# Loads of k and q ahead of the centroids, a cleared tile for the first idle products, and a shorter norm

## The chip, the cores and the metric

The kernel runs on one core of a Trainium2 chip. TensorE (PE), VectorE (DVE), ScalarE (ACT), GpSimd (POOL) and SyncE (SP) each take their own list of instructions in order and wait for each other through semaphores. The metric is the device time of one execution in microseconds, as a median over runs; less is better.

## What is computed

Clustered attention, followed by two dense blocks. Each query and key is assigned to the centroid whose direction is nearest; a query attends only to keys of its own cluster.

```python
B, H, S, D = 2, 8, 768, 64          # 16 clusters per head
c_n = centroids / (norm(centroids) + 1e-06)
q_assign = argmax(einsum('bhsd,hcd->bhsc', q_n, c_n))    # k_assign the same way
mask = q_assign[:, :, :, None] == k_assign[:, :, None, :]
scores = where(mask, q @ k.T / sqrt(D), -1e9)
x = softmax(scores) @ v             # then heads side by side: 1536 x 512
x = leaky(x @ moe_w_in) @ moe_w_out         # max(0.01 h, h)
x = relu(x @ moe2_w_in)**2 @ moe2_w_out
```

## The kernel before

Inputs come two heads at a time: a pair p holds q and k as tiles `rqk` (128 partitions: two heads of 64 dimensions; 768 columns) and v as `rv`. There are 8 pairs. Matrix products run in fp32 split into a rounded part and the rest, so that three products make one. Attention runs in units of 256 queries; the order of all engines in the attention is written out by hand in strings such as `RAMP` (the start) and `PLAN` (the steady part). The dense blocks follow, where TensorE has work all the time.

The change lies in the first microseconds, before `RAMP` begins. In the order of the program:

- GpSimd makes the identity `ident`, small constants (`eps`, `msc`, `mbi`, written at lines 156 to 166), a bf16 copy `identb` (L168), the cleared block tile `cbd` (L170), the ranks `desc` and padding.
- SyncE loads the centroids `ct` (L326), then k, q of pair 0 and q, k of pair 1 (`loads_qk`, L323, four transfers of 384 KB), then v (L318) and five copies between on-chip tiles (L694).
- `warm_up(9)` puts nine idle 128x128 products of `ident` on TensorE (L331); their result is not used. An fp32 product is two passes on TensorE, so nine of them show as 18.
- `prep_centroids` norms the centroids: squares and sums on VectorE (L335, L337), the square root on ScalarE (L339, behind a load of its function table), a load of the table for exp with a dummy step (L340), then on VectorE a floor of 1e-30 (L341), a reciprocal, one refining step and the scaling of `ct` (L343 to L351). TensorE transposes `ct` (L353), and ScalarE copies the two halves into `cbd` (L355, L356).
- `warm_up(3)` puts three more idle products behind the transpose.
- `head_0` makes the split operands of head 0 from k and q on VectorE and ScalarE (L712 to L729; `hb`). Then `RAMP` begins: `dK` and `dQ` multiply k and q with `cbd` (`dots`, L391, six products each), `fill` adds idle products (L774), `choose` finds each row's best cluster on VectorE (L782, L785, tile `pads`), `mask_mm` transposes that (L799, `ohT`), and the scores S (L521) follow.

All engines' order in this part is that of the code.

Of the kernel before, what the change touches and what calls it, by code (L numbers as in the profile page):

```python
# [8 lines left out]
F32 = mybir.dt.float32  # L9
# [5 lines left out]
AF = mybir.ActivationFunctionType  # L15
ALU = mybir.AluOpType
# [87 lines left out]
def attention_moe_moe_kernel(  # L104
# [9 lines left out]
    nc = tc.nc  # L114
# [35 lines left out]
    const = ast.enter_context(tc.tile_pool(name="const", bufs=1))  # L150
    const.tile([128, 120], F32, name="cpad")

    ident = const.tile([128, 128], F32, name="ident")
    make_identity(nc, ident)
    eps = const.tile([128, 1], F32, name="eps")
    nc.gpsimd.memset(eps, 1e-9)
    msc = const.tile([128, 1], F32, name="msc")
    mbi = const.tile([128, 1], F32, name="mbi")
    nc.gpsimd.memset(msc[0:32], BIG)
# [7 lines left out]
    identb = const.tile([128, 128], BF16, name="identb")  # L167
    nc.gpsimd.tensor_copy(out=identb, in_=ident)  # L168
    cbd = const.tile([128, HP, 2 * C], F32, name="cbd")
    nc.gpsimd.memset(cbd, 0.0)  # L170
    desc = const.tile([128, 24, C], F32, name="desc")
    for c in range(C):
        nc.gpsimd.memset(desc[:, :, c], float(2 ** (C + 8 - c)))
# [149 lines left out]
            nc.sync.dma_start(out=rqks[p][:, j], in_=qk[p, j])  # L323

    ct = const.tile([128, D], F32, name="ct")
    nc.sync.dma_start(out=ct, in_=cen)  # L326

    def warm_up(n):
        w = ps_t.tile([128, 512], F32, tag="T", name="warm")
        for i in range(n):  # L330
            nc.tensor.matmul(out=w[:, 0:128], lhsT=ident, rhs=ident, start=True, stop=True)  # L331

    def prep_centroids():
        sq = const.tile([128, D], F32, name="sq")
        nc.vector.tensor_tensor(out=sq, in0=ct, in1=ct, op=ALU.mult)  # L335
        ss = const.tile([128, 1], F32, name="ss")
        nc.vector.tensor_reduce(out=ss, in_=sq, axis=AX.X, op=ALU.add)  # L337
        n0 = const.tile([128, 1], F32, name="n0")
        nc.scalar.activation(out=n0, in_=ss, func=AF.Sqrt)  # L339
        nc.scalar.activation(out=const.tile([128, 1], F32, name="tab"), in_=eps, func=AF.Exp)  # L340
        nc.vector.tensor_scalar(out=n0, in0=n0, scalar1=1e-30, scalar2=None, op0=ALU.max)  # L341
        rn = const.tile([128, 1], F32, name="rn")
        nc.vector.reciprocal(out=rn, in_=n0)  # L343
        nc.vector.scalar_tensor_tensor(
            out=n0, in0=ss, scalar=rn, in1=n0, op0=ALU.mult, op1=ALU.add
        )
        nc.vector.tensor_scalar(
            out=n0, in0=n0, scalar1=0.5, scalar2=1e-6, op0=ALU.mult, op1=ALU.add
        )
        nc.vector.reciprocal(out=rn, in_=n0)  # L350
        nc.vector.tensor_scalar(out=ct, in0=ct, scalar1=rn, scalar2=None, op0=ALU.mult)  # L351
        ctp = ps_t.tile([128, 512], F32, tag="T", name="ctp")
        nc.tensor.transpose(ctp[0:64, 0:128], ct, ident)  # L353
        cview = ctp[0:64, 0:128].rearrange("p (a h c) -> p a h c", h=2, c=C)
        nc.scalar.copy(out=cbd[0:64, :, 0:C], in_=cview[:, :, 0])  # L355
        nc.scalar.copy(out=cbd[64:128, :, C : 2 * C], in_=cview[:, :, 1])  # L356
# [336 lines left out]
    for h, j in ((2, 3), (0, 2), (0, 3), (1, 2), (1, 3)):  # L693
        nc.sync.dma_start(  # L694
            out=heads[h][80:128, j].bitcast(F32), in_=heads[2][80:128, 2].bitcast(F32)
        )
    warm_up(9)
    prep_centroids()
    eighth = const.tile([128, 1], F32, name="eighth")
    warm_up(3)  # L700

    for h in range(2):
        hbs[h] = heads[h]
# [206 lines left out]
    for op in RAMP.split():  # L910
        if ":" in op:
            name, i = op.split(":")
            step(name, int(i), unit_ops[name])
        elif "@" in op:
            name, i = op.split("@")
# [6 lines left out]
    for u in range(-1, NU + 5):  # L922
# [9 lines left out]
        for op in PLAN[u % UPP].split():  # L932
            if ":" in op:
                name, lag = op.split(":")
                i = u - int(lag)
                if 0 <= i < NU:
                    step(name, i, unit_ops[name])
            else:
                name, ahead = op.split("@")
# [6 lines left out]
        w = u - (NU - UPP)  # L946
# [610 lines left out]
```

## Time and profile before

| what | value |
|---|---|
| median of 3 runs | 733.88 us (733.5 to 734.03) |
| profiled execution | 734.87 us, its span 733.1 us |
| TensorE busy | 725.6 us, 99% of the span |
| chain that ended last | TensorE 91%, VectorE 4%, ScalarE 2%, GpSimd 1% |

The span is the time from the first to the last instruction of the profiled execution. The chain is followed back from the last instruction: at each step to what released it, or to the instruction ahead on its engine. A start time in the rows counts from the span's start.

### The profile page before, as it was taken

The numbers are of one execution on the slowest core, as the hardware profiler recorded it, in microseconds if no ns is written. First come the engines' busy times: TensorE is split into PE (matmuls) and PEld (weight loads), VectorE is DVE, ScalarE is ACT, GpSimd is POOL, SyncE is SP. The second block draws the span as 40 slices with busy tenths as digits, with TensorE's granted clock in tenths as the row PEclk, the third lists the DMA queues.
The fourth block names the chain that finished last, engine by engine and source line by source line (L and its number), as shares of the span: only waits on it lengthen the run. The fifth ranks groups of instructions, "written<-read, shape, count | busy, mean of one in ns | idle before, by whom it ended". The sixth has DMA issues, their size and how long they took to land.

```text
span 733.1 us, 11920 instructions
## 1 busy us (share of the span) xinstructions
PE 725.6 (99%) x4246; PEld 644.4 (88%) x4246; DVE 562.3 (77%) x893; ACT 500.0 (68%) x923; POOL 596.5 (81%) x562
## 2 busy tenths in 40 slices
PE   9999999999999999999999999999999999999997
PEld 8999999999998888888888888888888898888986
DVE  7989999999998737686776866887677595775946
ACT  7978988988998777447365464658847558375561
POOL 6999999999959977987787877899798786787840
PEclk9999999999999999999999999999999999999999
DMA  5693573662611312212121131111113112121004
GB/s 150 161 219 104 128 172 104 136 167 66 146 54 59 115 58 79 94 58 97 56 79 57 58 115 58 59 58 58 58 59 114 59 58 79 64 89 57 1 1 173
DMA packets 17756, 65.58 MB, mean 89 GB/s; under 512 B 3120, under 2 KB 6320, under 8 KB 12704
## 3 DMA queue, kind: packets, MB, share of 16 engines
q1 hardware_dynamic: 17696, 64.81, 30.0%
q8 instruction: 34, 0.56, 0.3%
q14 instruction: 26, 0.21, 0.1%
HBM read 43.02 MB, written 3.15 MB: 63 GB/s over the span
## 4 chain that ended last, share of the span: by engine, by line
PE 91%; DVE 4%; ACT 2%; POOL 1%; issue 1%; DMA 1%; ACTq 0%; DVEq 0%; POOLq 0%
PE h L1043 33%; PE o L1274 18%; PE h L1274 10%; PE A L618 8%; PE S L521 7%; PE T L583 7%; PE o L1121 4%; PE S L391 2%; DVE nm L543 1%; ACT e L553 1%; DVE el L600 1%; PE warm L331 1%; DMA out<-q 1%; POOL e L570 0%; PE dots L391 0%
## 5 line engine op out<-in xcount | busy, mean ns | idle before, releaser
L1043 PE MATMUL h<-xh,wh 128*128 128x512 f32 x272 | 106.7, 392 | 0.0
L1043 PE MATMUL h<-xh,wl 128*128 128x512 f32 x272 | 106.1, 390 | 0.0
L1043 PE MATMUL h<-xl,wh 128*128 128x512 f32 x272 | 106.1, 390 | 0.0
L1228 POOL TENSOR_TENSOR gl<-t,gh 128x512 fp32r<-128x512 f32 x56 | 79.9, 1444 | 31.9 <-ACT gh L1225 21.9
L197 POOL TENSOR_TENSOR wl<-ws,wh 128x1024 fp32r<-128x1024 f32 x28 | 67.8, 2420 | 41.8 <-ACT wh L194 41.8
L570 POOL TENSOR_SCALAR e<-e,r 128x768 f32<-128x768 f32 x96 | 87.4, 919 | 12.5 <-PE T L583 6.8
L600 DVE TENSOR_TENSOR el<-T,eh 128x512 fp32r<-128x512 f32 x144 | 94.6, 683 | 3.0 <-ACT eh L594 1.9
L543 DVE TENSOR_REDUCE nm<-S 128x1 f32<-128x768 f32 x96 | 90.9, 949 | 3.9 <-PE S L391 2.5
L553 ACT ACTIVATE e<-S,nm 128x768 f32<-128x768 f32 x96 | 87.3, 910 | 9.6 <-DVE nm L543 5.8
L521 PE MATMUL S<-hb 128*128 128x384 f32 (+1 forms) x384 | 89.6, 347 | 1.6 <-ACT eh L594 0.4
L594 ACT CAST eh<-T 128x512 fp32r<-128x512 f32 x144 | 79.7, 590 | 9.6 <-PE T L583 9.4
L1173 DVE TENSOR_TENSOR h<-h,q 128x512 f32<-128x512 f32 x42 | 29.4, 699 | 70.6 <-PE h L1043 45.3
L197 POOL TENSOR_TENSOR wl<-wt,wh 128x1024 fp32r<-128x1024 f32 x31 | 75.5, 2434 | 9.6 <-ACT wh L194 8.7
L618 PE MATMUL A<-eh,vv 128*128 128x256 f32 x288 | 80.2, 307 | 0.0
L583 PE MATMUL T<-ident,e 128*128 128x128 f32 x576 | 79.5, 273 | 0.0
L618 PE MATMUL A<-el,vv 128*128 128x256 f32 x288 | 73.0, 283 | 0.0
L583 PEld LDWEIGHTS T<-ident,e 128*128 128x128 f32 x576 | 68.9, 143 | 3.0
L224 ACT ACTIVATE wt<-wraw 128x1024 f32<-128x1024 f32 (+1 forms) x33 | 36.8, 1115 | 47.5 <-POOL ws L286 47.3
L521 PEld LDWEIGHTS S<-hb 128*128 128x128 f32 (+1 forms) x384 | 62.2, 189 | 3.7 <-ACT e L553 1.9
L1228 DVE TENSOR_TENSOR gl<-h,gh 128x512 fp32r<-128x512 f32 x70 | 48.0, 688 | 18.3 <-ACT h L1210 7.9
L1043 PEld LDWEIGHTS h<-xh,wh 128*128 128x128 f32 x272 | 51.1, 188 | 11.6 <-DVE gl L1228 1.1
L1043 PEld LDWEIGHTS h<-xh,wl 128*128 128x128 f32 x272 | 51.0, 188 | 10.6
(202 smaller groups left out, 2088.3 us busy)
## 6 DMA issues: line engine op xcount, KB each, us to landing
wraw<-w SPq DMA_DIRECT2D x32, 1024.0 KB, 4.7
hb<-spl SPq DMA_DIRECT2D x14, 576.0 KB, 4.7
hb<-spl SPq DMA_DIRECT2D x42, 192.0 KB, 5.1
rqk<-qk SPq DMA_DIRECT2D x16, 384.0 KB, 3.7
rv<-v SPq DMA_DIRECT2D x8, 384.0 KB, 3.4
out<-q SPq DMA_DIRECT2D x11, 256.0 KB, 2.2
hb<-st SPq DMA_DIRECT2D x56, 24.0 KB, 2.1
hb<-hb SPq DMA_DIRECT2D x5, 144.0 KB, 7.0
```

The lines of the kernel that those rows point to most:

```text
L197: last_of["wl"] = eng.tensor_tensor(out=wl, in0=t, in1=wh.bitcast(F32), op=ALU.subtract).ins
L521: nc.tensor.matmul(out=s[:, c, 0:HALF], lhsT=hb[0:k, a, i * 128 : (i + 1) * 128], rhs=hb[0:k, b, c * HALF : (c + 1) * HALF], start=(a == 0 ...
L543: last_of["nm", t] = nc.vector.tensor_reduce(out=n, in_=s_t[t][:, :, 0:HALF], axis=AX.XY, op=ALU.max, negate=True).ins
L553: nc.scalar.activation(out=e.rearrange("p (a b) -> p a b", a=2), in_=s_t.pop(t)[:, :, 0:HALF], func=AF.Exp, bias=n_t.pop(t), scale=1.0, ac ...
L570: last_of["norm"] = nc.gpsimd.tensor_scalar(out=e_t[t], in0=e_t[t], scalar1=r_t[t // 2][:, t % 2 : t % 2 + 1], scalar2=1.0, op0=ALU.mult, ...
L583: nc.tensor.transpose(T[:, o : o + 128], e_t[2 * u + b][:, kc * 128 : (kc + 1) * 128], ident)
L594: last_of["eh", u, g] = nc.scalar.copy(out=eh[:, 2 * g : 2 * g + 2, :].rearrange("p a b -> p (a b)"), in_=T_t[u, g]).ins
L600: last_of["el"] = last_of["el", u, g] = nc.vector.tensor_tensor(out=el[:, 2 * g : 2 * g + 2, :].rearrange("p a b -> p (a b)"), in0=T_t.pop ...
L618: nc.tensor.matmul(out=A, lhsT=w, rhs=m[:, kc, :], start=(kc == 0 and i == 0), stop=(kc == KC - 1 and i == 1),)
L1043: nc.tensor.matmul(out=out, lhsT=l, rhs=r, start=(first and i == 0), stop=(i == n - 1), skip_group_check=not first,)
L1228: eng.tensor_tensor(out=lo[n], in0=full[n], in1=hi[n].bitcast(F32), op=ALU.subtract)
L1274: nc.tensor.matmul(out=out, lhsT=l, rhs=r, start=(fresh and i == 0), stop=(stop and i == 2), skip_group_check=True,)
```

## The change

The centroids' load is issued by ScalarE, not SyncE, so k and q stand first on SyncE's queue. `cbd` is cleared by VectorE, not GpSimd, and the first two idle products multiply this cleared tile with itself; five with `ident` and three with `identb` (bf16) follow, in place of nine with `ident`. Behind the transpose six bf16 idle products stand in place of three fp32 ones. The floor of 1e-30 under the norm becomes a bias of 1e-30 under the square root, from a new tile `tiny` that GpSimd writes.

```diff
+    tiny = const.tile([128, 1], F32, name="tiny")
+    nc.gpsimd.memset(tiny, 1e-30)
...
-    nc.gpsimd.memset(cbd, 0.0)
+    nc.vector.memset(cbd, 0.0)
+    flat_cbd = cbd.rearrange("p h c -> p (h c)")
...
-    nc.sync.dma_start(out=ct, in_=cen)
-
-    def warm_up(n):
+    nc.scalar.dma_start(out=ct, in_=cen)
+
+    def warm_up(*todo):
         w = ps_t.tile([128, 512], F32, tag="T", name="warm")
-        for i in range(n):
-            nc.tensor.matmul(out=w[:, 0:128], lhsT=ident, rhs=ident, start=True, stop=True)
+        for x, n in todo:
+            for i in range(n):
+                nc.tensor.matmul(out=w[:, 0:128], lhsT=x, rhs=x, start=True, stop=True)
...
-        nc.scalar.activation(out=n0, in_=ss, func=AF.Sqrt)
+        nc.scalar.activation(out=n0, in_=ss, func=AF.Sqrt, bias=tiny)
         nc.scalar.activation(out=const.tile([128, 1], F32, name="tab"), in_=eps, func=AF.Exp)
-        nc.vector.tensor_scalar(out=n0, in0=n0, scalar1=1e-30, scalar2=None, op0=ALU.max)
...
-    warm_up(9)
+    warm_up((flat_cbd, 2), (ident, 5), (identb, 3))
     prep_centroids()
     eighth = const.tile([128, 1], F32, name="eighth")
-    warm_up(3)
+    warm_up((identb, 6))
```

ScalarE at the program's start, before; in brackets the semaphores that a row waits for, by the engine or DMA that raises them:

```order
L339 ACT_TABLE_LOAD
L339 ACTIVATE n_193<-ss 128x1 [waits DVE_49]
L340 ACT_TABLE_LOAD
L340 ACTIVATE tab<-eps 128x1 [waits Pool_49]
L355 COPY cbd<-ctp 64x4x16 [waits PE_49,Pool_49]
```

ScalarE at the same place, now (the lines of the changed kernel stand three or four further down):

```order
L329 DMA ct<-cen 128x64
L343 ACT_TABLE_LOAD [waits DVE_49]
L343 ACTIVATE n_196<-ss,tiny 128x1 [waits Pool_49]
L344 ACT_TABLE_LOAD
L344 ACTIVATE tab<-eps 128x1
L358 COPY cbd<-ctp 64x4x16 [waits PE_49]
```

The centroids' DMA is ScalarE's first instruction, and the wait for VectorE's sum, which stood at the square root, now stands ahead of the table load.

TensorE from its first product to the first dots, before:

```order
L331 MATMUL warm<-ident 128x128 [waits Pool_49]
L331 MATMUL warm<-ident 128x128 x8
L353 MATMUL ctp<-ident,ct 64x128 [waits DVE_49]
L331 MATMUL warm<-ident 128x128 x3
L391 MATMUL dots<-cbd,rqk 128x32 [waits PE_49,DMAHW1_49,Activation_49,Pool_49]
```

TensorE at the same place, now; the two rows on `identb` come three times ahead of the transpose `ctp`, and six times behind it:

```order
L335 MATMUL warm<-cbd 128x128 [waits DVE_49]
L335 MATMUL warm<-cbd 128x128
L335 MATMUL warm<-ident 128x128 [waits Pool_49]
L335 MATMUL warm<-ident 128x128 x4
L335 LDWEIGHTS identb [waits Pool_49]
L335 MATMUL warm<-identb 128x128
...
L356 MATMUL ctp<-ident,ct 64x128 [waits DVE_49]
...
L394 MATMUL dots<-cbd,rqk 128x32 [waits DMAHW1_49,PE_49,Activation_49]
```

The first products wait for VectorE's cleared tile and no longer for GpSimd's identity; in fp32 passes there are 14 ahead of the transpose where there were 18, and three short products.

## Rows read from the trace of the kernel before

**Rows 1.** The page's first and fourth part: busy time, and the chain.

```profile
PE 725.6 (99%) x4246; PEld 644.4 (88%) x4246; DVE 562.3 (77%) x893; ACT 500.0 (68%) x923; POOL 596.5 (81%) x562
PE 91%; DVE 4%; ACT 2%; POOL 1%; issue 1%; DMA 1%; ACTq 0%; DVEq 0%; POOLq 0%
```

**Rows 2.** The chain in order of time, start: start us, us, what.

```profile
1.41 4.21 PE warm L331 x18
5.62 0.21 PE ctp L353
5.84 1.04 PE warm L331 x6
6.88 1.26 PE dots L391 x12
```

**Rows 3.** Timeline of SyncE: start us, us, instruction.

```profile
0.74 0.38 SPq L326 DMA_DIRECT2D ct<-cen  x1
1.17 1.84 SPq L323 DMA_DIRECT2D rqk<-qk  x4
```

**Rows 4.** Timeline of VectorE; in brackets its idle time, and what ended it.

```profile
2.42 0.23 DVE L335 TENSOR_TENSOR sq<-ct 128x64 f32<-128x64 f32 x1 [2.42 <-DMA ct<-cen]
2.68 0.22 DVE L337 TENSOR_REDUCE ss<-sq 128x1 f32<-128x64 f32 x1
3.17 0.15 DVE L341 TENSOR_SCALAR n<-n 128x1 f32<-128x1 f32 x1 [0.27 <-ACT n L339]
3.36 0.16 DVE L343 RECIPROCAL rn<-n 128x1 f32<-128x1 f32 x1
...
4.20 0.26 DVE L351 TENSOR_SCALAR ct<-ct,rn 128x64 f32<-128x64 f32 x1
5.18 0.55 DVE L714 TENSOR_SCALAR hb<-rqk 64x768 fp32r<-64x768 f32 x1 [0.73 <-DMA rqk<-qk]
...
7.23 0.95 DVE L725 SCALAR_TENSOR_TENSOR hb<-rqk,hb 64x768 fp32r<-64x768 f32 x1
8.21 0.36 DVE L782 TENSOR_REDUCE m<-dots 128x12 f32<-128x192 f32 x1
...
9.48 0.84 DVE L782 TENSOR_REDUCE m<-dots 128x12 f32<-128x192 f32 x2
```

**Rows 5.** Timeline of ScalarE.

```profile
0.73 1.28 ACT L339 ACT_TABLE_LOAD   x1 [0.73 <-PEq L1547]
2.94 0.20 ACT L339 ACTIVATE n<-ss 128x1 f32<-128x1 f32 x1 [0.92 <-DVE ss L337]
3.16 1.28 ACT L340 ACT_TABLE_LOAD   x1
4.45 0.20 ACT L340 ACTIVATE tab<-eps 128x1 f32<-128x1 f32 x1
5.93 0.21 ACT L355 COPY cbd<-ctp 64x64 f32<-64x64 f32 x1 [1.28 <-PE ctp L353]
```

**Rows 6.** Timeline of TensorE: weight loads, and the first dots.

```profile
5.21 0.18 PEld L353 LDWEIGHTS ctp<-ident,ct 128*64 128x64 f32 x1
6.72 1.42 PE L391 MATMUL dots<-cbd,rqk 128*128 128x32 f32 x12
```

**Rows 7.** Groups of ScalarE's steps to 18 us: shapes, count | busy us, mean ns.

```profile
L339 ACT ACTIVATE n<-ss 128x1 f32<-128x1 f32 x1 | 0.2, 204 | 0.9 <-DVE ss L337 0.9
L564 ACT ACTIVATE r<-r,eps 128x2 f32<-128x2 f32 x1 | 0.3, 298 | 0.0
```

**Rows 8.** Stretches: busy time by engine, granted clock, DMA engines' busy share, GB/s.

```profile
1.75:2.00 0.25, 0.25 (x2) 0.25 (x2) 0.00 (x0) 0.25 (x1) 0.19 (x3) 1.00 0.51 116
2.00:2.25 0.25, 0.25 (x3) 0.25 (x3) 0.00 (x0) 0.01 (x1) 0.25 (x2) 1.00 0.88 59
...
3.00:3.50 0.50, 0.50 (x5) 0.50 (x3) 0.29 (x2) 0.48 (x2) 0.44 (x8) 1.00 0.74 98
```

**Rows 9.** Timeline of GpSimd: the clearing of the block tile.

```profile
2.17 0.21 POOL L170 MEMSET cbd<- 128x128 f32 x1
```

**Rows 10.** Timeline of TensorE later: three bf16 products.

```profile
27.65 0.33 PE L473 MATMUL ohT<-identb,oh 128*128 128x128 bf16 x3
```

**Rows 11.** Products of one line (ns min/median/max); weight loads 5.6:6.4, 6.6:8.

```profile
L331 PE MATMUL warm<-ident x24: 275/421/582, 1.4 to 6.6; 128*128 128x128 f32 x24
...
L331 PEld LDWEIGHTS warm<-ident 128*128 128x128 f32 x5 | 1.2, 327 | 0.0
...
L391 PEld LDWEIGHTS dots<-cbd,rqk 128*128 128x128 f32 x12 | 1.4, 192 | 0.0
```

**Rows 12.** Waits up to 12.6 us: who for whom, us, times, longest.

```profile
POOL qs L748 <- ACT eighth L729: 4.0, 1, 4.0
```

## The prediction

> **What bounds the kernel now.** I read the page first. TensorE is busy for 99% of the span and carries 91% of the chain of work that ended last [rows 1], so once the pipeline is full nothing outside TensorE can be made late or early by much without the end moving with it. The change touches the first 10 us alone, so the question is what sets the start. The chain in order of time [rows 2] says: idle products from 1.41 to 5.62 us, the centroid transpose, idle products again to 6.88, then the dot products of head pair 0 and the masks. A chain through TensorE's queue names the instruction ahead, even when that one is only padding, so I looked at who was ready when.
>
> Four lanes meet there. (a) The centroids: issued at 0.74, landed 1.7 us later, normed on VectorE from 2.42 to 4.46 with one step on ScalarE between [rows 3 to 5]. (b) TensorE: nine fp32 idle products stand ahead of the transpose, whose weight load starts only at 5.21 [rows 6], 0.75 us after the centroids were ready. That is the loss which the change goes for. (c) k: VectorE's first use of it, L714, starts at 5.18 and waited 0.73 us for its DMA [rows 4]. (d) After that VectorE runs L714, L721, L714, L725 without a gap to 8.18 and reduces the first dots at 8.21 [rows 4]; TensorE's first twelve dot passes end at 6.72 + 1.42 = 8.14 [rows 6]. So VectorE and TensorE arrive together: an edit has to bring both forward to gain, and delays if it pushes back either.
>
> **Part 1, the norm of the centroids.** L341 goes: from its start at 3.17 to the next at 3.36 is **0.19 us saved** [rows 4]. In its place the square root takes its bias from a tile. A ScalarE step on 128x1 without one took 204 ns, L564 with a bias tile took 298 [rows 7]: **+0.09**, bounds 0 and 0.10 since L564 has two elements a row.
>
> The larger cost is in the order of ScalarE's instructions. The square root now waits for two engines (VectorE for the sum, GpSimd for the new tile). Before, the table load L339 stands ahead of any wait, ran from 0.73 to 2.01 and was over 0.92 us before the sum came [rows 5]. In the changed order the wait for VectorE stands ahead of the table load, which can thus start only when the sum is there. The cover of that load was the centroids' transfer; it is gone. Price: **+1.28 us** [rows 5] and about 0.05 for the extra waiting step (this is the idle between neighbours such as 2.90 and 2.94). Part 1 in sum: 1.28 + 0.05 + 0.09 - 0.19 = +1.23. With the centroids landing as before the centroid tile is ready at 4.46 + 1.23 = 5.69 instead of 4.46.
>
> On that load: the row shows 1.28 us, and the step behind the second load starts 0.01 us after it (3.16 + 1.28 = 4.44, then 4.45) [rows 5]. The Trainium skill (ScalarE: Activation LUTs, What ACT_TABLE_LOAD costs) states the same 1283 ns but adds a drain of some 1380 ns for every switch. By that rule the sum would be about 1.4 us longer; no such drain shows here, so I leave it out.
>
> **Part 2, the queues.** SyncE spends 0.43 us between the start of the centroids' DMA and the next one (0.74 to 1.17) [rows 3]. k, q and all behind them go out 0.43 earlier; k lands at about 4.75 instead of 5.18. That is worth 0.43 only while VectorE is free to take it; by part 1 it is not.
>
> The centroids now leave on ScalarE's queue at about 0.73, when its first instruction could start [rows 5], so at the same moment as k, and not ahead of it. No DMA of the trace goes out on ScalarE's queue. Lower bound of the added delay: 0. The centroids' bytes moved before 2.0 us (116 GB/s for a quarter of a microsecond is their 32 KB), and k, issued at 1.17, moved next to nothing until 2.0 [rows 8]; 0.43 earlier it would only begin to. Upper bound: they land with k, 4.75 - 2.4 = 2.3 us late, since the DMA engines are already 74 to 88% busy at 59 to 98 GB/s in several stretches from 2.0 to 3.5 [rows 8], a sign of slow first packets. I take **+0.2**, near the lower end, because the nearest row, the centroids' own transfer, was over before k could have been in its way.
>
> **Part 3, the idle products.** The cleared tile is now written by VectorE as its first work. The trace has no VectorE memset; GpSimd's of the same tile took 0.21 [rows 9], VectorE's step on half as many elements 0.26 [rows 4]. So TensorE begins near 1.0 instead of 1.41. Seven fp32 products are 14 passes; eighteen stood between 1.41 and the transpose's load at 5.21, 0.21 each [rows 6]: until about 4.0. Three bf16 products add 0.3 to 0.65 (later in the kernel three of them span 0.33 [rows 10]; twice that as the other bound, since the fp32 loads are up to 1.7 times slower in this stretch than behind it [rows 11]). TensorE is free for the transpose at 4.3 to 4.6, so this edit does what it says. But the centroid tile is there at 5.7 to 5.9, and TensorE **pauses for over 1 us**.
>
> **The sum.** VectorE: 5.69 + 0.2 = 5.89 plus the usual 0.03 gives L714 at 5.92 against 5.18, +0.74. ScalarE and TensorE: transpose from 5.9; the first product of a row of them takes 0.58 at this clock [rows 11], so the copies into the block tile start at 6.55 instead of 5.93 and the dots at about 7.05 instead of 6.72, +0.3, as six bf16 products (0.3 to 0.65) no longer stand in the way. VectorE is the later of the two. Two reduces at L782 share a row of 0.84 us from 9.48 [rows 4]; the second waits for the second dots, and each lasts 0.36, so some 0.1 to 0.2 us there is waiting that VectorE's delay uses up. That leaves **+0.5 us** at the mask transposes. From there the chain [rows 2] alternates DVE, ACT, POOL and PE with issue gaps of 0.03 to 0.1 and hardly any slack; GpSimd and ScalarE start their own lanes behind the same copies (L748 waits for L729, 4.0 us) [rows 12], so all lanes shift together. I take the whole +0.5 to the end: span 733.6, and against the median, which is 0.99 below the profiled execution's 734.87, 733.88 + 0.5 = **734.4**. Without the 0.2 for the queue 734.2, with 0.6 for it 734.8.
>
> **Rivals.** (1) *The table load is hidden after all*: the chip starts it while the wait is pending. Then the centroid tile is ready at 4.46 - 0.19 + 0.09 + 0.2 = 4.6, the transpose runs at once, dots start at 5.8, and k at 4.75 sets VectorE: -0.43, **733.45**. Against it: the second load, L340, stands behind a step that waited until 2.94 and did not start before 3.16 [rows 5].
> (2) *The centroids queue behind k*: each DMA engine serves both queues in turns, and k's first packets are slow [rows 8]. Taking half to two thirds of the upper bound, they land 1.1 to 1.5 us late in place of 0.2; the sum grows by 0.9 to 1.3, **735.5**. It decides, for a loss over 0.2%, from 1.2 us on. The Trainium skill (DMA: Bandwidth & Descriptors, Queues, rings and completion order) speaks for it: an engine takes packets from its queues by turns. No run so far shows two queues at once.
> (3) *The clock rises later* (slower). The granted-clock column reads 1.00 throughout [rows 8], but the same 128x128 fp32 weight load takes 327 ns in the idle products up to 6.4 us and 192 in the dots behind 6.6 [rows 11]: TensorE ran at the lower level, 1.2 GHz, for some 5 us of work without a pause and then rose to 2.4. With a pause from 4.5 to 5.9 the rise may miss the dots. A pass then takes 0.21 instead of 0.12 (1.42 us for twelve [rows 6]): the first twelve dots cost 1.1 on top of their 0.3, the fills and the second twelve half as much again and more. TensorE then binds instead of VectorE, +1.4 to +2.9 in all: 735.3 to 736.8, **735.7** where the rise falls between the two sets of dots. For it: the pause; against it: TensorE starts 0.4 us sooner and is busy again before 6.6.
> (4) *Absorbed*: some later wait swallows the shift, **733.9**.
>
> **Chances.** Forecast 0.42, (1) 0.10, (2) 0.14, (3) 0.22, (4) 0.12. A measurement can tell about 0.2%, 1.5 us, from no change. Faster by that much needs more than (1) can give: 0.03. Slower by that much is 0.6 of (2), 0.65 of (3) and a tail of the forecast: 0.25. The rest, 0.72, is within. Range 733.2 to 736.0: it holds the forecast, (4), most of (1) and (2) and the cheaper half of (3).
>
> **What would show it.** In the changed profile the first table load should start near 2.95 or later, behind L341's reduce, and not at 0.73; the centroid tile ready at 5.6 to 5.9; TensorE idle for a microsecond or more ahead of the transpose; L717 (now k's first use) waiting for VectorE's own work, not for the DMA; k landed near 4.75. If the table load still stands at 0.73, (1) holds. If the centroids land at 3.4 or later, (2). If the weight loads of the dots take over 300 ns, (3). If L717 is 0.7 late and the exps of the first unit are not, (4).

## The result, and the profile after

The changed kernel takes 740.5 us (median; 739.74 to 741.15) against 733.95 in the same comparison: 1.0085 times as long, 95% interval 1.0074 to 1.0096, or **6.5 us slower**. The forecast was 734.4, +0.5 us, within 733.2 to 736.0, with a chance of 0.72 that the change is too small to be told; the measured time lies far outside. The profiled execution took 739.74 us, with a span of 738.0. It lies only 4.9 us above the profiled one of the kernel before, because that one (734.87) was 0.9 slower than this comparison's median.

The loss is there before the attention has begun. The first row maximum (L543, now L546) starts at 19.88 us instead of 14.00; the first product of the dense blocks is 5.3 us late (234.8 for 229.5 us). These are the two lanes that lead to it, first ScalarE of the changed kernel, from the timeline (start us, us, instruction; idle time and what ended it in brackets), to be held against [rows 5]:

```profile
0.73 0.40 ACTq L329 DMA_DIRECT2D ct<-cen  x1
4.79 1.28 ACT L343 ACT_TABLE_LOAD   x1 [4.79 <-DVE ss L341]
6.09 0.29 ACT L343 ACTIVATE n<-ss,tiny 128x1 f32<-128x1 f32 x1
6.40 1.28 ACT L344 ACT_TABLE_LOAD   x1
...
8.03 0.20 ACT L358 COPY cbd<-ctp 64x64 f32<-64x64 f32 x1
```

The table load waits for VectorE's sum, as its place in the order said, and costs its 1.28 us behind it. But the sum itself is late. VectorE's timeline, against [rows 4]:

```profile
4.23 0.23 DVE L339 TENSOR_TENSOR sq<-ct 128x64 f32<-128x64 f32 x1 [3.23 <-DMA ct<-cen]
4.49 0.22 DVE L341 TENSOR_REDUCE ss<-sq 128x1 f32<-128x64 f32 x1
6.42 0.16 DVE L346 RECIPROCAL rn<-n 128x1 f32<-128x1 f32 x1 [1.71 <-ACT n L343]
...
7.26 0.25 DVE L354 TENSOR_SCALAR ct<-ct,rn 128x64 f32<-128x64 f32 x1
7.43 0.55 DVE L717 TENSOR_SCALAR hb<-rqk 64x768 fp32r<-64x768 f32 x1
...
11.31 0.36 DVE L785 TENSOR_REDUCE m<-dots 128x12 f32<-128x192 f32 x1 [0.90 <-PE dots L394]
```

The centroids land at 4.2 us instead of 2.4. The tile is ready at 7.51 instead of 4.46: 1.81 us for the transfer and 1.25 for the norm. The last row shows a third thing: VectorE, itself over 2 us late, has to wait another 0.9 us for the dots. TensorE's timeline says why, against [rows 6]:

```profile
7.57 0.42 PE L356 MATMUL ctp<-ident,ct 128*64 128x128 f32 x1 [2.84 <-DVE ct L354]
7.78 0.85 PE L335 MATMUL warm<-identb 128*128 128x128 bf16 x6
8.50 2.77 PE L394 MATMUL dots<-cbd,rqk 128*128 128x32 f32 x12
11.08 1.20 PE L777 MATMUL dots<-ident 128*128 128x128 f32 x4
12.08 2.61 PE L394 MATMUL dots<-cbd,rqk 128*128 128x32 f32 x12
...
17.63 0.61 PE L777 MATMUL dots<-ident 128*128 128x128 f32 x4
```

After a stop of 2.84 us the same twelve passes take 2.77 us instead of 1.42, and four fills 1.20; at 17.63 four fills take 0.61 again. The groups of weight loads (count | busy us, mean ns), up to 16.9 us and from 17.6 us on, confirm it with one and the same load:

```profile
L394 PEld LDWEIGHTS dots<-cbd,rqk 128*128 128x128 f32 x24 | 5.3, 332 | 0.1
...
L394 PEld LDWEIGHTS dots<-cbd,rqk 128*128 128x128 f32 x24 | 2.9, 192 | 0.0
```

These 332 ns are the lower level, 1.2 GHz, that [rows 11] show for the idle products (327 ns there), and 192 the upper, 2.4 GHz. The clock rose at about 17.2 us here; in the kernel before it rose at about 6.5. (The granted-clock column reads 1.00 in this whole stretch, although the same load takes 332 ns in one part of it and 192 in the other. So it is the loads that tell the level ahead of the first change that the column shows.)

The chain, in order of time, adds up. Its main pieces, against [rows 2]:

```profile
0.73 3.48 DMA ct<-cen
4.79 1.28 ACT L343
...
8.63 2.64 PE dots L394 x12
11.27 1.01 PE dots L777 x4
12.29 2.40 PE dots L394 x12
14.69 1.01 PE dots L777 x4
15.70 0.64 PE S L524 x2
16.34 1.46 PE ohT L802 x9
...
19.88 0.97 DVE nm L546
```

The last row stood at this place in the chain of the kernel before:

```profile
14.00 0.97 DVE nm L543
```

In the kernel before, the dots were 1.26 each in that chain, so 2.5 us of the 5.9 at the first row maximum lie in the two dozens of dots alone, and the fills, the first scores and the masks lie in the same slow stretch. The transpose starts 2.15 us later (7.57 for 5.42), and its idle products are 0.4 shorter. The rest, 5.9 - 2.15 + 0.4 = 4.1 us, lies in that slow stretch. What remained to be shown was whether the stop makes the clock late, or the late centroids, the zeros or the bf16.

### The profile page after: what moved, and what is told of

It is laid out like the page before. It is cut to its first block, busy times and chain, and to the rows that moved or that the text cites. A ratio compares the mean times of both kernels' runs of the same rounds, so it can differ in the third digit from the quotient of the medians.

```text
span 738.0 us, 11917 instructions
## 1 busy us (share of the span) xinstructions
PE 728.6 (99%) x4245; PEld 646.9 (88%) x4245; DVE 561.9 (76%) x893; ACT 499.0 (68%) x923; POOL 595.8 (81%) x562
## 4 chain that ended last, share of the span: by engine, by line
PE 90%; DVE 4%; ACT 3%; POOL 1%; DMA 1%; issue 1%; ACTq 0%; DVEq 0%; POOLq 0%
PE h L1046 33%; PE o L1277 18%; PE h L1277 10%; PE A L621 8%; PE S L524 7%; PE T L586 7%; PE o L1124 4%; ACT e L556 2%; PE S L394 2%; DVE nm L546 1%; DVE el L603 1%; PE dots L394 1%; ACT eh L597 1%; DMA out<-q 1%; DMA ct<-cen 0%
## 5 line engine op out<-in xcount | busy, mean ns | idle before, releaser
L546 DVE TENSOR_REDUCE nm<-S 128x1 f32<-128x768 f32 x96 | 90.9, 948 | 3.7 <-PE S L394 2.3
```

The source lines that it names most:

```text
L546: last_of["nm", t] = nc.vector.tensor_reduce(out=n, in_=s_t[t][:, :, 0:HALF], axis=AX.XY, op=ALU.max, negate=True).ins
```

## The experiments

Medians in us; "before" is the kernel before on the same chip in the same comparison. The changed kernel's 740.5 stood against 733.95, and the runs below against 733.81 to 734.24, so what a run takes back of the 6.5 us is known to about 0.3.

| run | this | range of executions | before | interval of the ratio |
|---|---|---|---|---|
| a1_norm_back | 739.48 | 739.3 to 740.5 | 734.24 | 1.0058 to 1.0088 |
| a2_ct_on_sync | 736.94 | 736.5 to 737.9 | 734.24 | 1.0023 to 1.0053 |
| a3_idle_back | 740.5 | 740.2 to 741.1 | 734.24 | 1.0071 to 1.0104 |
| a4_pause_filled | 735.02 | 734.9 to 736.4 | 734.24 | 1.0007 to 1.0026 |
| b1_norm_only | 734.42 | 733.8 to 735.0 | 734.23 | 0.9993 to 1.0012 |
| b2_queue_only | 736.35 | 734.7 to 740.0 | 734.23 | 1.0015 to 1.0054 |
| b3_idle_only | 733.65 | 732.9 to 738.4 | 734.23 | 0.9984 to 1.0012 |
| b4_fewer_idle | 738.48 | 738.3 to 738.8 | 734.23 | 1.0038 to 1.0068 |
| c1_table_first | 734.05 | 733.6 to 734.8 | 734.07 | 0.9994 to 1.0011 |
| c2_sync_filled | 735.2 | 734.0 to 735.9 | 734.07 | 1.0007 to 1.0025 |
| c3_idle_fp32 | 733.78 | 732.9 to 734.4 | 734.07 | 0.9987 to 1.0005 |
| c4_queue_filled | 735.09 | 734.2 to 735.4 | 734.07 | 1.0004 to 1.0022 |
| d1_sync_filled_more | 734.42 | 733.3 to 734.8 | 733.81 | 0.9995 to 1.0013 |

### One part of the change undone

**The norm.**

```diff
-        nc.scalar.activation(out=n0, in_=ss, func=AF.Sqrt, bias=tiny)
+        nc.scalar.activation(out=n0, in_=ss, func=AF.Sqrt)
...
+        nc.vector.tensor_scalar(out=n0, in0=n0, scalar1=1e-30, scalar2=None, op0=ALU.max)
```

> The changed kernel with the norm as it was (the floor under the norm back, no bias tile). Theory: three delays add up, the centroids landing 1.8 us late, the table load of 1.28 us behind the wait, and TensorE's clock rising only at 17.2 us. Undoing the norm alone puts the table load back to 0.73 us and the centroid tile to about 6.3 us instead of 7.5; TensorE still pauses some 1.6 us ahead of the transpose. If the clock still rises late: about 739.3 us, 1.2 below the changed kernel. Rival, that the table load is what costs nearly all: about 735. Rival, that a pause of this length leaves the clock alone: about 736.

739.48, near the first figure: 1.0 to 1.3 us of the 6.5. The table load is hidden again (it starts at 1.17, behind the issue of the centroids' DMA), the centroid tile ready at 6.1, and TensorE stops 1.46 us; its dots still take 2.77 us a dozen.

**The queue.**

```diff
-    nc.scalar.dma_start(out=ct, in_=cen)
+    nc.sync.dma_start(out=ct, in_=cen)
```

> The changed kernel with the centroids' load back as SyncE's first DMA. Theory: they land at 2.4 us again, the table load (still behind the wait) makes the centroid tile ready at about 5.7, TensorE pauses about 1 us. This is the case that the prediction priced at 734.2 us with the clock on time. If the clock rises late all the same, the dots run at half speed: about 737 to 738.5. Rival, that the queue alone makes the loss: 734.

736.94: 3.6 to 3.9 us of the 6.5, yet 2.7 above the kernel before. Stretches of this run (busy time by engine, then the granted clock, DMA share, GB/s):

```profile
4.60:7.80 3.20, 1.94 (x20) 1.68 (x19) 2.98 (x9) 3.15 (x6) 0.00 (x0) 1.00 0.84 256
8.00:14.60 6.60, 6.60 (x31) 6.30 (x32) 4.03 (x11) 3.13 (x7) 5.53 (x4) 0.50 0.63 167
15.00:18.00 3.00, 3.00 (x26) 2.69 (x24) 2.37 (x5) 2.89 (x5) 0.70 (x1) 1.00 0.03 5
```

The clock had risen early here. TensorE then stood idle from 4.67 to 5.76, and the granted clock fell to half, 1.2 GHz, from about 8 to 14.6 us, while TensorE was busy. Its timeline shows the stop, a first dozen of dots at the upper level and a second at the lower:

```profile
5.76 0.30 PE L356 MATMUL ctp<-ident,ct 128*64 128x128 f32 x1 [1.09 <-DVE ct L354]
...
6.57 1.59 PE L394 MATMUL dots<-cbd,rqk 128*128 128x32 f32 x12 [0.18 <-ACT cbd L359]
...
8.97 2.61 PE L394 MATMUL dots<-cbd,rqk 128*128 128x32 f32 x12
```

So a rise that has come is not safe either: behind a stop it was lost again, some 2 us after the stop had ended. All four executions show it in their mean granted clock: it is 0.995, as 6.6 us of 735 at half clock make it.

**The idle products.**

```diff
-    nc.vector.memset(cbd, 0.0)
+    nc.gpsimd.memset(cbd, 0.0)
...
-    warm_up((flat_cbd, 2), (ident, 5), (identb, 3))
+    warm_up((ident, 9))
...
-    warm_up((identb, 6))
+    warm_up((ident, 3))
```

> The changed kernel with the idle products as before (nine of the fp32 identity ahead of the transpose, three behind, the block tile cleared by GpSimd). The centroid tile is still ready at 7.5 us; the idle products end at 5.6, so TensorE pauses 1.9 us instead of 2.8. Theory, that the pause keeps the clock down: still late, 739 to 740.5. Rival, that the zeros or the bf16 products keep it down: the clock rises near 6.5 us and the time falls to about 736.

740.5, no gain at all. Nine fp32 products end at 5.45 us while the centroid tile comes at 7.51: the stop is still 2.1 us. The loss is there without zeros and without bf16, so they are not its cause. The stretches show the same fall as above (1.00, then 0.50 from 8.6 to past 18):

```profile
5.20:8.50 3.30, 1.19 (x10) 0.90 (x9) 1.91 (x7) 3.19 (x7) 0.00 (x0) 1.00 1.01 320
8.60:12.00 3.40, 3.40 (x17) 3.40 (x18) 2.50 (x5) 3.34 (x6) 1.75 (x2) 0.50 0.85 141
12.00:18.00 6.00, 6.00 (x29) 5.68 (x29) 2.70 (x8) 1.43 (x3) 3.74 (x3) 0.50 0.02 6
```

**The stop filled, all else as changed.**

```diff
-    warm_up((flat_cbd, 2), (ident, 5), (identb, 3))
+    warm_up((flat_cbd, 2), (ident, 14), (identb, 3))
```

> The changed kernel with nine more idle fp32 products ahead of the transpose, so that TensorE has no pause until the centroid tile is ready at 7.5 us. Theory: the clock rises near 6.5 us as in the kernel before, the dots take 1.4 us a dozen again, and what is left is VectorE's delay of 2.2 us: 736. So the pause is worth some 4.4 us of the 6.5. Rival, that the late centroids cost all by themselves: 739 or more.

735.02: nine idle products that compute nothing take back 5.5 to 5.8 of the 6.5 us (eight of ten executions lie at 734.9 to 735.1, two at 736.4). TensorE's timeline, to be held against the changed kernel's above:

```profile
2.07 5.17 PE L335 MATMUL warm<-ident 128*128 128x128 f32 x28
...
7.58 0.30 PE L356 MATMUL ctp<-ident,ct 128*64 128x128 f32 x1 [0.18 <-DVE ct L354]
...
8.39 1.53 PE L394 MATMUL dots<-cbd,rqk 128*128 128x32 f32 x12 [0.18 <-ACT cbd L359]
...
10.28 1.42 PE L394 MATMUL dots<-cbd,rqk 128*128 128x32 f32 x12
```

The centroids are as late as in the changed kernel (transpose at 7.58), but the dots take 1.53 and 1.42 us. So a centroid tile 3 us late costs 0.8 us by itself; I had put that at 2. The first row maximum is 2.0 us late (16.03 us) and the dense blocks start 1.5 us late, so the ramp absorbs a part.

### One part of the change alone

**The norm alone.** The edit is a1's, the other way round, on the kernel before.

> The kernel before with the norm's edit alone. The table load moves behind the wait and the centroid tile is ready at 5.7 us instead of 4.46. The nine idle products last until 5.6, so TensorE hardly pauses. Theory: clock on time, +0.3 to +0.6 us, 734.3. Rival, that any lateness of the centroids lets the clock rise late: +1.5 or more.

734.42, as expected, and not told from no change. The table load stands exposed here too, but the nine idle products cover it (stop 0.15 us); the first row maximum is 0.2 us late (14.23). ScalarE, timeline:

```profile
3.01 1.28 ACT L341 ACT_TABLE_LOAD   x1 [3.01 <-DVE ss L339]
4.31 0.29 ACT L341 ACTIVATE n<-ss,tiny 128x1 f32<-128x1 f32 x1
```

**The queue alone.** The edit is a2's, the other way round.

> The kernel before with the queues' edit alone (centroids from ScalarE, k first on SyncE). The centroids land at 4.2 us instead of 2.4, the tile is ready at 6.3; the table load stays hidden. Idle products last until 5.6, a pause of 0.7 us. Theory, with the clock on time: VectorE +1.1, in all +0.8 to +1.1, 734.9. If 0.7 us of pause is enough to delay the clock: 736 or more.

Both happened. Of ten executions five lie at 734.7 to 735.2, two at 737.5 and 737.6, three at 739.4 to 740.0, so the median is the middle of a gap. The stop is 1.16 us; the profiled execution was one of the quick ones and its clock was up. The other five have no profile, but their mean granted clock is on record: 0.995 in the two, as in a2, where a risen clock was lost again, and 1.000 in the three. That fits a clock which came up late, as in the changed kernel's profiled execution, whose mean reads 1.000 too because the column misses a level that is low from the start. To see whether the clock makes the spread, the stop was filled:

```diff
-    warm_up(9)
+    warm_up(12)
```

> The kernel before with the queues' edit alone, as one run had it (734.7 to 740.0 from execution to execution), and three more idle products, so that the pause of 1.2 us ahead of the transpose is filled. Theory: the spread was the clock, met or missed by the pause; filled, all executions lie near 734.8, the price of centroids that land 1.8 us late. Rival, that the queue edit itself spreads the time: 735 to 740 again.

735.09, and all eleven executions within 734.2 to 735.4. The spread is gone, and +1.0 us is the queue edit's own price. The queues' rows of the changed kernel from 1 to 5 us (packets, MB, share; then KB each, us to landing) show both queues at work, q1 with the loads that SyncE issues and q10 with the centroids:

```profile
q1 hardware_dynamic: 359, 1.00, 73.2%
q10 hardware_dynamic: 144, 0.03, 3.8%
...
ct<-cen ACTq DMA_DIRECT2D x1, 32.0 KB, 3.5
```

First on SyncE, the same 32 KB landed 1.7 to 1.8 us after their issue in all nine traces; from ScalarE, beside k's 384 KB, they took 3.3 to 3.5 in all six. In the changed kernel they landed at 4.2, when k itself was there at 4.0. All 144 packets of q10 moved between 2.0 and 4.0 us, and 200 of q1 in the same time; in the kernel before 130 of them had moved by 2.0. So the centroids shared the DMA engines with k's load all the way. No run loads them from ScalarE with k out of the way, so it is not shown how much of the 1.8 us ScalarE's queue would take by itself.

**The idle products alone.** The edits to `cbd`, `warm_up` and its two calls.

> The kernel before with the idle products' edit alone. The centroid tile is ready at 4.46 us, the idle products end at 4.7: no pause. Transpose 0.7 us sooner, VectorE as before (k lands at 5.16). Theory: 733.5 to 734, as before. Rival, that products of zeros or of bf16 count for less with the clock: it rises later and the time grows by 1 to 3 us.

733.65, like the kernel before, but one execution of ten at 738.36. In the profiled execution TensorE had no stop of note, and still the clock fell for a while, a fall that cost little. So a stop is not the only thing that can lose a risen clock:

```profile
6.00:8.80 2.80, 2.80 (x27) 2.80 (x27) 2.56 (x6) 2.74 (x6) 1.47 (x2) 1.00 0.83 289
9.20:12.20 3.00, 3.00 (x15) 2.68 (x15) 1.75 (x6) 1.33 (x4) 2.83 (x3) 0.50 0.94 170
12.60:15.00 2.40, 2.40 (x19) 2.12 (x18) 2.05 (x4) 2.35 (x4) 0.87 (x2) 1.00 0.18 47
```

The same with fp32 in place of bf16:

```diff
-    warm_up((flat_cbd, 2), (ident, 5), (identb, 3))
+    warm_up((flat_cbd, 2), (ident, 6))
...
-    warm_up((identb, 6))
+    warm_up((ident, 3))
```

> The kernel before with the idle products begun on the cleared tile, two of it and six of the fp32 identity ahead of the transpose and three fp32 behind, none in bf16. Theory: like the run with the idle edit alone, 733.3 to 733.8, but without its rare slow executions (one of ten at 738.4) if it is the short bf16 products that let the clock go. Rival: rare slow executions here too, because TensorE then gets ahead of VectorE and pauses at the masks.

733.78 and none of eleven above 734.4. One in ten against none in eleven does not settle whether bf16 is the reason; that stays open.

### The stop by itself, and the forecast by itself

**A stop put into the kernel before.**

```diff
-    warm_up(9)
+    warm_up(4)
```

> The kernel before with four idle products ahead of the transpose in place of nine. Nothing else moves: the centroid tile is ready at 4.46 us, the idle products end near 3.3, so TensorE pauses 1.2 us and is then free 0.75 us sooner than before. Theory, that a pause delays the clock: the dots run at half speed, 735.5 to 737. Rival, that the pause does no harm by itself: 733.5 to 733.9.

738.48, **4.2 us slower**, with nothing late by more than 0.1 us: less work on TensorE, the centroid tile ready at 4.56 and the transpose 0.8 us sooner than before. TensorE's timeline:

```profile
1.41 2.07 PE L331 MATMUL warm<-ident 128*128 128x128 f32 x8 [1.41 <-POOL ident masks.py:199]
4.61 0.42 PE L353 MATMUL ctp<-ident,ct 128*64 128x128 f32 x1 [1.13 <-DVE ct L351]
...
6.11 2.61 PE L391 MATMUL dots<-cbd,rqk 128*128 128x32 f32 x12
```

A stop of 1.13 us, and the dots take 2.61 us a dozen; the clock comes up only at about 16 us, although TensorE works without a stop from 4.61 on. So a stop is enough for the slow clock, with no late centroids and no other edit; they matter mostly because they make one. (A stop and fewer idle products are one thing here: no run keeps the stop and adds work elsewhere.)

**The case that the forecast described**: table load behind the wait, centroids first on SyncE, no stop. First with eight `ident` products in place of five, then with twelve and four fp32 products behind the transpose.

> The changed kernel with the centroids back first on SyncE and three more fp32 idle products, so that TensorE has no pause before the centroid tile is ready at 5.7 us. This is the case that the prediction took as its forecast, with the clock on time and the table load behind the wait: 734.2 by its sum. Theory, that the pause of 1.1 us in the run with the queue undone cost its 2.7 us: 734 to 734.5. Rival, that the late table load is dear by itself: over 735.5.

735.2, in two clusters, 734.0 to 734.5 and 735.2 to 735.9. Two stops were left (0.68 us ahead of the transpose, 0.18 ahead of the dots). The mean granted clock parts the clusters: 0.999 to 1.000 in the five executions of the quick one, 0.997 to 0.998 in the six of the other. With the clock kept this case thus took +0.3.

> The changed kernel with the centroids back first on SyncE and twelve fp32 idle products in place of five ahead of the transpose, four fp32 in place of six bf16 behind it, so that neither of the two stops of TensorE that the run with eight of them still had (0.7 and 0.2 us) is left. Theory: that run's two clusters of times (734.0 to 734.5 and 735.2 to 735.9) were the clock, kept or lost for a while; without a stop all executions lie at 734.0 to 734.7, the prediction's own forecast. Rival, that the table load behind the wait costs 1.1 us by itself: 735.2 again.

734.42, 0.6 above the 733.81 of its own comparison, with no execution above 734.8. The idle products outlast the centroid tile here (it is ready at 5.78, the transpose starts at 7.00), so part of the 0.6 is theirs. Together with b1 (+0.2) and the quick cluster of c2 (+0.3) this fits the +0.3 that the prediction gave for the case without the queue; but b1 and d1 are not told from no change, so the runs bear the sum out only in that they leave no room for much more.

**A version that might beat both.** A dummy square root ahead of the real one brings the table load back to the front; the idle products begin on the cleared tile, all others fp32; the centroids stay first on SyncE.

```diff
+        nc.scalar.activation(out=const.tile([128, 1], F32, name="pre"), in_=eps, func=AF.Sqrt)
         nc.scalar.activation(out=n0, in_=ss, func=AF.Sqrt, bias=tiny)
```

> The kernel before with the shorter norm, but with a dummy square root on ScalarE ahead of it, so that the table load runs before the wait; the idle products begin on the cleared tile (two of it, six of the fp32 identity, three fp32 behind the transpose); the centroids stay first on SyncE. Theory: the table load starts at 0.73 us again, the centroid tile is ready at 4.4, the idle products end at 4.6 to 4.8 without a pause, the clock rises on time: 733.2 to 733.8, 0.5 to 1 below the kernel before. Rival, that the early stage has no slack left to give: 734.2. Rival, that it pauses later and loses the clock: over 736 in some executions.

734.05, the same as before: the rival. The table load starts at 0.73 again and the first row maximum is 0.7 us sooner (13.3 for 14.0) in the profiled executions, but that is not seen at the end. No run was told apart from the kernel before on the quick side.

## Why the prediction was wrong, step by step

**What bounds the start: half right.** That two lanes meet and both have to move was right. I read the idle products as padding ahead of the transpose, "the loss which the change goes for". They were the cover that brings the clock up; b4 takes five of them away and loses 4.2 us. And lane (c), VectorE's wait of 0.73 us for k, belongs to the one execution that I read: k landed 4.0 us after its issue there, and 3.1 to 3.4 us after it in all fourteen other traces. With k there at about 4.5, VectorE's 3.0 us of work would end at about 7.5 (an estimate from [rows 4]), 0.6 ahead of TensorE's dots at 8.14, so the two need not arrive together.

**Part 1, the norm: right.** The load moved behind the wait, took 1.28 us, and the step with the bias tile 0.29 instead of 0.20. Measured +1.25 on the centroid tile, summed +1.23. The step behind the load starts within 0.02 us of its end, twice; the further drain of the Trainium skill (ScalarE: Activation LUTs, What ACT_TABLE_LOAD costs) shows in none of these traces, and its sum would have been too long.

**Part 2, the queue: the term that was mis-sized.** I took +0.2 between bounds of 0 and 2.3; it measured +1.81. The value was taken near the lower end because the centroids' own transfer, in the kernel before, was over before k's bytes moved. That row shows the transfer ahead of k on the engines, which is what the edit ended; with both issued at 0.73 the row that mattered was k's. The rule of the Trainium skill that I weighed as a rival (DMA: Bandwidth & Descriptors, Queues, rings and completion order: an engine takes packets from its queues by turns) agrees with the measured landing, 4.2 us beside k's 4.0, and by it the term belongs at the upper end. k landed at 4.0, sooner than the 4.75 summed, since the 5.18 that I started from was a late one; its gain was worth nothing, as forecast.

**Part 3, the idle products, and the sum: right on the edit, wrong on the stop.** They began at 1.05 and ended at 4.72, a little behind the 4.3 to 4.6 summed. I saw a stop of over 1 us and priced it at nothing in the sum; it was 2.84 us. This is the step that failed most: "VectorE is the later of the two" took the dots at the upper level of the clock, where they would end with VectorE. At the lower level they took 2.77 us a dozen, VectorE waited 0.90 us for the first and 1.78 for the second, and TensorE set the start. Filling the stop took back 5.5 to 5.8 of the 6.5 us (a4).

**The rivals: each there, taken one at a time.** The late centroids (2) and the late clock (3) were each given a chance as if only one could come, 735.5 and 735.7. But (2) lengthens the stop that makes (3), and (3) came already in the forecast's own case: with a stop of 1.1 us, a2 lost the clock in all four executions. Both signs that the prediction had set came, the centroids behind 3.4 us and the dots' loads over 300 ns; together the two had no price in the text. Rival 3's price was too low as well: its sum let the clock rise between the dots or soon behind; it stayed down to 17.2 us, over the fills, the first scores and the masks, and cost 4 to 5.8 us.

**The way to the end: nearly right.** I took shifts at the masks to pass in full. The 5.9 us at the first row maximum came out as 5.3 at the dense blocks; with the clock kept, 2.0 became 1.5, and 0.8 in the median (a4).

## What to carry to other kernels

Before an idle product at the start is taken away or moved, ask what TensorE does until the next real one: at the start a stop of 1.1 us cost 4.2 us here (b4), far more than the wait that one sees in the chain. Rivals that share a cause belong together: when one of them makes another likelier, price the two in a sum. And when a transfer is moved to a second queue to go out at the same moment as a larger one, reckon with the larger one's landing as its own. Last, a wait that one execution shows is worth holding against a second trace before a sum is built on it.

## What the runs showed of the hardware that I had not expected

Behind a stop of about a microsecond a rise that had already come was lost: 1.00 in 4.6 to 7.8 us, then 0.50 from 8.0 to 14.6 with TensorE busy all that time (a2). The rise itself does not come at a fixed moment: with the same nine idle products from 1.41 us on, the loads fell from 333 to 192 ns at about 6.5 us in the kernel before, 5.0 in a3 and 4.6 in b2. A small DMA on a second queue landed later than one of twelve times its size that was issued with it (4.2 against 4.0 us). And the outcome of a stop of 1.16 us was not the same from execution to execution (734.7 to 740.0 in b2), while one of 1.13 us, with less work ahead of it, cost 4.1 to 4.6 us in all four executions (b4). Whether it is the moment of the rise that decides between them was not tried.
